# A gap of 64 bytes between the ring of the split weights and the activations

## The chip, the core and the metric

The kernel runs on one core of a Trainium2 chip. The metric is the device time of one execution in microseconds (us); lower is better. TensorE multiplies and writes to PSUM, VectorE, ScalarE and GpSimd work on vectors, and SyncE issues DMAs. A matmul has two operands in SBUF: the weights, 128 x 128 here, which an instruction of their own loads into the array, and the columns, 256 or 512 of them, which stream through it. Both lie at byte addresses within each of SBUF's 128 partitions, and those addresses are what this change is about.

## What is computed

```python
attn_out = _attn_ref(q, k, v, n_sink, window)          # 2 x 8 heads, 768 x 64, window 128, 4 sinks
x = attn_out.transpose(0, 2, 1, 3).reshape(1536, 512)
h = x @ w_in                                           # 512 -> 2048
y = (max(h, 0) + alpha * min(h, 0)) @ w_out            # 2048 -> 512
p = domain_probs / (domain_probs.sum(-1) + 1e-09)
out = sum(p[:, e] * (max(y @ w1[e], 0) @ w2[e]) for e in range(4))   # 512 -> 1024 -> 512
```

All arrays are float32. To keep that precision the kernel splits every operand of the feed-forward part into a high and a low half of a shorter float format (names ending in h and l) and makes three matmuls of one product: high by high, high by low, low by high.

## The kernel before

**Stages.** Attention runs over 32 pairs of a head with 256 queries, one per step p. From step 11 on, the first layer of the feed-forward part is interleaved with it by a hand-written list (`LEAD`): for units of 256 tokens and single blocks of 128 features, `s1` (x into the hidden block) and later `s2_transposed` (hidden block into the output). Each of the two is a burst of 12 matmuls of 256 columns. Then `rest` finishes the first layer: one more unit of 256 tokens, then the other blocks for chunks of 512 tokens, again 12 matmuls for `s1` and 12 for `s2_transposed`, now of 512 columns. Last come the experts. Their first pair of blocks goes through `s1` and `s2_natural`; the other 15 pairs go through `products`, which makes seven products of half size instead of eight: `four` for tokens 0 to 1023 (48 matmuls of 512 columns), `halves` for tokens 1024 to 1535 (42 matmuls of 256 columns), and then `out` (72 matmuls of 512 columns).

**Which operand is which.** In `s1` and `products` the weights of the matmul are slices of the split weights (`wh`, `wl`, and `th`, `tl` for sums of them), the columns are x (`xh`, `xl`, later called `yh`, `yl` in the same tiles) or sums of x (`s2h` and the like in pool `wide`; `s_wh`, `s_wl` in the trace are the sums for `halves`, which lie in the right-hand pools below). In `s2_transposed` the weights are again from `wh`, `wl`, the columns are the hidden block (`gha`, `gla`, `gh`, `gl`). In `s2_natural` and `out` it is the other way round: the weights of the matmul are slices of the hidden block (`hgh`, `hgl`), and the columns are the second half of `wh`, `wl`.

**Addresses.** They follow from the order and size of the tiles, and the compiled program has the same ones. Pools are stacked from the left. `base` ends at byte 33,792 of a partition, which is 264 x 128. Pool `accp` (called `work`) follows: three accumulators of 8,192 bytes, two tiles `cm` of 2,048, the ring of six `wh` and six `wl` of 4,096, then three `xh` and three `xl` of 8,192. On top of it lie `at` and `tmp` during attention (with `ptsb`, `p`, `v`, `gha`, `gla`), and later `wide` (sums of x, `gh`, `gl`, `hgh`, `hgl`). Every size and every slice used by a matmul of the feed-forward part is a multiple of 128, so all these operands begin at a multiple of 128 bytes. From the right end hang `top` with a pad of 32 bytes and, below it, the two pools `late`, which hold the weights of blocks 6, 7, 14 and 15 (line 119 decides: slot k % 8 of 6 or 7) and later `s_wh`, `s_wl`; and, during attention, `atk` with `qs`, `kh`, `kl`. All of these begin 64 bytes past a multiple of 128 (221,120, 225,216, 212,928 and 217,024 for the four weights' tiles). The small tiles `ident` and `warm` in `base` begin 32 bytes past one.

In this document the **distance** of a matmul is the start of its columns minus the start of its weights, modulo 128: 0 for two operands in the same half of 128 bytes, 64 for opposite halves.

Of the kernel before, what the change touches and what calls it, by code (L numbers as in the profile page):

```python
# [9 lines left out]
F32 = mybir.dt.float32  # L10
# [11 lines left out]
P = 128  # L22
# [32 lines left out]
class Body:  # L55
# [643 lines left out]
        nc.gpsimd.tensor_tensor(lo, x, hi.bitcast(F32), ALU.subtract)  # L699

    def new_x(self, c, name="x"):
        self.xh[c] = self.work.tile([P, DM // P, CH], F32R, tag="xh", name=f"{name}h{c}", bufs=NC)
        self.xl[c] = self.work.tile([P, DM // P, CH], F32R, tag="xl", name=f"{name}l{c}", bufs=NC)

# [349 lines left out]
```

## Time and profile before

| | us |
|---|---|
| median of 3 runs | 895.2 (894.92 to 896.19) |
| the profiled execution, whole | 895.68 |
| its span, first to last instruction | 893.9 |
| TensorE busy in it (4956 matmuls) | 881.4 |

The profile has one line per group of equal instructions, and a timeline with the start of each. TensorE's matmuls overlap: the duration of one (389 ns for 512 columns) counts from its first column to its last result, and the next one starts before that. What a matmul costs in a dense run is therefore not its duration but the **step**, the time from its start to the start of the next one, and steps are read from starts in the timeline. The granted clock of TensorE is 0.998 of full speed over the span.

### The profile page before, as it was taken

To read this page: it belongs to the slowest core of one execution; us is meant where nothing else is said; L and a number is where in the kernel's file an instruction comes from. 1 tells how busy PE (TensorE), PEld (TensorE's weight loads), DVE (VectorE), ACT (ScalarE), POOL (GpSimd) and SP (SyncE) were. 2 spreads that over 40 slices of the span, in tenths; PEclk is the share of its full clock that TensorE was granted. 3 is DMA by queue.
4 is the path that set the end of the run, shared out by engine and by line. 5 is a ranking of instruction groups with operands and counts; after the bars stand their busy time and mean duration, and the time that the engine had idled before them with its cause. 6 is when DMAs were issued, how large, how long until landed. Compare 5 with 4: busy or idle time off the path is not lost.

```text
span 893.9 us, 13192 instructions
## 1 busy us (share of the span) xinstructions
PE 881.4 (99%) x4956; PEld 747.4 (84%) x4956; DVE 560.0 (63%) x1104; ACT 330.8 (37%) x773; POOL 368.9 (41%) x349
## 2 busy tenths in 40 slices
PE   9999999999999999999999999999999999999997
PEld 6578899998888888888888888888888888888886
DVE  5778877657995553456655665665566556656654
ACT  4787766754431222233312321231233223212310
POOL 1366644535763454475224404421441344044210
PEclk9999999999999999999999999999999999999999
DMA  5754432302332020000011101101110111011003
GB/s 163 190 184 146 154 120 84 100 1 71 119 118 71 12 70 13 1 25 23 1 48 48 41 7 48 48 3 46 47 48 1 48 48 36 12 48 48 1 1 146
DMA packets 23722, 54.51 MB, mean 61 GB/s; under 512 B 3168, under 2 KB 3168, under 8 KB 23648
## 3 DMA queue, kind: packets, MB, share of 16 engines
q1 hardware_dynamic: 23504, 53.57, 19.0%
q8 instruction: 41, 0.67, 0.3%
q14 instruction: 33, 0.27, 0.1%
q10 hardware_dynamic: 144, 0.00, 0.0%
HBM read 50.42 MB, written 3.15 MB: 60 GB/s over the span
## 4 chain that ended last, share of the span: by engine, by line
PE 93%; DVE 4%; issue 1%; ACT 1%; POOL 0%; DVEq 0%; ACTq 0%; POOLq 0%
PE o L437 9%; PE o L436 9%; PE o L438 9%; PE h L374 5%; PE h L375 5%; PE h L376 5%; PE h L253 5%; PE h L254 5%; PE h L255 5%; PE o L262 5%; PE o L263 5%; PE o L264 5%; PE pv L676 3%; PE c L374 3%; PE c L376 3%; PE c L375 3%
## 5 line engine op out<-in xcount | busy, mean ns | idle before, releaser
L441 DVE SCALAR_TENSOR_TENSOR acc<-o,prob,acc 128x512 f32<-128x512 f32 x180 | 135.1, 751 | 100.3 <-PE o L438 100.3
L140 POOL TENSOR_TENSOR wl<-wraw,wh 128x512 fp32r<-128x512 f32 x60 | 76.6, 1297 | 280.8 <-ACT wh L139 280.8
L437 PE MATMUL o<-wl,hgh 128*128 128x512 f32 x240 | 93.5, 389 | 0.0
L438 PE MATMUL o<-wh,hgl 128*128 128x512 f32 x240 | 93.4, 389 | 0.0
L436 PE MATMUL o<-wh,hgh 128*128 128x512 f32 x240 | 93.4, 389 | 0.0
L253 PE MATMUL h<-xh,wh 128*128 128x256 f32 (+1 forms) x264 | 90.1, 341 | 0.0
L254 PE MATMUL h<-xl,wh 128*128 128x256 f32 (+1 forms) x264 | 87.6, 332 | 0.0
L255 PE MATMUL h<-xh,wl 128*128 128x256 f32 (+1 forms) x264 | 87.4, 331 | 0.0
L289 POOL TENSOR_TENSOR gl<-qk,gh 128x512 fp32r<-128x512 f32 (+1 forms) x36 | 49.5, 1375 | 70.9 <-ACT gh L288 68.7
L288 ACT ACTIVATE gh<-qk 128x512 fp32r<-128x512 f32 (+1 forms) x36 | 21.5, 598 | 122.5 <-DVE qk L287 119.8
L379 DVE TENSOR_TENSOR wraw<-h,wraw 128x512 f32<-128x512 f32 x45 | 31.1, 691 | 48.2 <-PE h L376 46.3
L382 ACT ACTIVATE wraw<-h 128x512 f32<-128x512 f32 x15 | 8.9, 596 | 140.7 <-PE h L376 140.7
L286 DVE TENSOR_SCALAR qk<-h,alpha 128x512 f32<-128x512 f32 (+1 forms) x36 | 25.3, 703 | 53.4 <-PE h L255 53.3
L263 PE MATMUL o<-gl,wh 128*128 128x512 f32 (+1 forms) x144 | 54.0, 375 | 2.5 <-POOL gl L289 2.5
L253 PEld LDWEIGHTS h<-xh,wh 128*128 128x128 f32 x264 | 49.9, 189 | 6.5 <-issue 1.7
L255 PEld LDWEIGHTS h<-xh,wl 128*128 128x128 f32 x264 | 49.9, 189 | 4.8
L254 PEld LDWEIGHTS h<-xl,wh 128*128 128x128 f32 x264 | 50.0, 189 | 4.5
L608 ACT ACTIVATE p<-p,nmax 128x288 f32<-128x288 f32 (+1 forms) x96 | 47.9, 501 | 15.8 <-DVE nmax L587 15.7
L262 PE MATMUL o<-gh,wh 128*128 128x512 f32 (+1 forms) x144 | 53.7, 373 | 0.0
L264 PE MATMUL o<-gh,wl 128*128 128x512 f32 (+1 forms) x144 | 53.4, 371 | 0.0
L438 PEld LDWEIGHTS o<-wh,hgl 128*128 128x128 f32 x240 | 45.0, 188 | 9.4
L436 PEld LDWEIGHTS o<-wh,hgh 128*128 128x128 f32 x240 | 45.0, 188 | 8.9
(209 smaller groups left out, 2440.7 us busy)
## 6 DMA issues: line engine op xcount, KB each, us to landing
wraw<-in_w SPq DMA_DIRECT2D x32, 512.0 KB, 3.6
wraw<-in_w SPq DMA_DIRECT2D x64, 256.0 KB, 2.9
qk<-in_qk SPq DMA_DIRECT2D x21, 352.0 KB, 3.0
v<-in_v SPq DMA_DIRECT2D x12, 256.0 KB, 3.4
out<-acc SPq DMA_DIRECT2D x12, 256.0 KB, 2.3
qk<-in_qk SPq DMA_DIRECT2D x8, 272.0 KB, 3.7
qk<-in_qk SPq DMA_DIRECT2D x11, 176.0 KB, 3.0
qk<-in_qk SPq DMA_DIRECT2D x8, 136.0 KB, 3.4
```

Source lines behind the costliest of these rows:

```text
L140: nc.gpsimd.tensor_tensor(lo, x, hi.bitcast(F32), ALU.subtract)
L253: mm(ps, wh[:, c], xh[:, dk, :], start=dk == 0, stop=False)
L254: mm(ps, wh[:, c], xl[:, dk, :], start=False, stop=False)
L255: mm(ps, wl[:, c], xh[:, dk, :], start=False, stop=dk == DM // P - 1)
L262: mm(outs[dt], wh[:, c], gh, start=first and begins[dt], stop=False, skip_group_check=True)
L263: mm(outs[dt], wh[:, c], gl, start=False, stop=False, skip_group_check=True)
L264: mm(outs[dt], wl[:, c], gh, start=False, stop=last, skip_group_check=True)
L374: mm(ps, bh[:, c], ah[:, d, :], start=first and d == 0, stop=False, skip_group_check=True)
L436: mm(ps, hh[:, n], wh, start=x == 0, stop=False)
L437: mm(ps, hh[:, n], wl, start=False, stop=False)
L438: mm(ps, hl[:, n], wh, start=False, stop=x == 1)
L441: nc.vector.scalar_tensor_tensor(acc, ps, self.prob[:, nt, e:e + 1], acc, ALU.mult, ALU.add)
```

## The change

A tile of 64 bytes is allocated right before the first tile of x, and never used. The branch runs once, for the first chunk of x. (`general` is the path for other masks, which isn't taken here.)

```diff
@@ -699,6 +699,9 @@
     def new_x(self, c, name="x"):
+        if name in "xg" and not self.xh:
+
+            self.work.tile([P, 16], F32, name="gap")
         self.xh[c] = self.work.tile([P, DM // P, CH], F32R, tag="xh", name=f"{name}h{c}", bufs=NC)
         self.xl[c] = self.work.tile([P, DM // P, CH], F32R, tag="xl", name=f"{name}l{c}", bufs=NC)
```

No instruction is added, removed or moved. Everything in `accp` from `xh` on, and all that is stacked on it (`at`, `tmp`, `wide`), moves up by 64 bytes. The accumulators, `cm`, the ring, `base` and everything on the right stay where they were.

## Rows read from the trace of the kernel before

**Rows 1.** The page: busy us (share) of engines; shares of the last chain by engine

```profile
PE 881.4 (99%) x4956; PEld 747.4 (84%) x4956; DVE 560.0 (63%) x1104; ACT 330.8 (37%) x773; POOL 368.9 (41%) x349
...
PE 93%; DVE 4%; issue 1%; ACT 1%; POOL 0%; DVEq 0%; ACTq 0%; POOLq 0%
```

**Rows 2.** TensorE by stage: stretch, busy us (instructions), granted clock, DMA share, GB/s

```profile
40.00:92.00 52.00, 49.89 (x400) 1.00 0.51 157
92.00:204.00 112.00, 112.00 (x988) 1.00 0.28 86
204.00:226.00 22.00, 19.55 (x163) 1.00 0.30 96
240.00:430.00 190.00, 190.00 (x838) 1.00 0.13 44
437.00:890.00 453.00, 451.48 (x2292) 1.00 0.11 37
```

**Rows 3.** Waits from 204 to 226 us: total us, times, longest

```profile
ACT gh L288 <- DVE qk L287: 6.7, 4, 2.1
...
PEld o L263 <- POOL gl L289: 3.1, 3, 1.1
```

**Rows 4.** Groups of matmuls by shape: busy us, mean ns of one, idle before

```profile
L437 PE MATMUL o<-wl,hgh 128*128 128x512 f32 x240 | 93.5, 389 | 0.0
...
L263 PE MATMUL o<-gl,wh 128*128 128x512 f32 x120 | 46.9, 391 | 0.0
...
L376 PE MATMUL c<-yh,wl 128*128 128x256 f32 x60 | 17.0, 283 | 0.0
...
L376 PE MATMUL c<-s_wh,tl 128*128 128x256 f32 x60 | 16.6, 277 | 0.0
```

**Rows 5.** Timeline of TensorE in the first layer: start us, duration us, matmul

```profile
251.47 0.39 PE L253 MATMUL h<-xh,wh 128*128 128x512 f32 x1
251.70 0.39 PE L254 MATMUL h<-xl,wh 128*128 128x512 f32 x1
...
254.22 0.39 PE L262 MATMUL o<-gh,wh 128*128 128x512 f32 x1
...
256.94 0.39 PE L253 MATMUL h<-xh,wh 128*128 128x512 f32 x1
...
259.69 0.39 PE L262 MATMUL o<-gh,wh 128*128 128x512 f32 x1
```

**Rows 6.** Timeline of one `halves`, 42 matmuls, and the start of `out`

```profile
466.82 0.28 PE L374 MATMUL c<-yh,wh 128*128 128x256 f32 x1
...
467.54 0.29 PE L374 MATMUL c<-s_wh,th 128*128 128x256 f32 x1
...
467.90 0.28 PE L374 MATMUL c<-s_wh,th 128*128 128x256 f32 x1
...
468.92 0.28 PE L374 MATMUL c<-yh,th 128*128 128x256 f32 x1
...
471.76 0.39 PE L436 MATMUL o<-wh,hgh 128*128 128x512 f32 x1
```

**Rows 7.** Timeline of one burst of 12 during attention, and two scores after it

```profile
153.52 0.36 PE L253 MATMUL h<-xh,wh 128*128 128x256 f32 x1
153.72 0.28 PE L254 MATMUL h<-xl,wh 128*128 128x256 f32 x1
...
154.91 0.28 PE L255 MATMUL h<-xh,wl 128*128 128x256 f32 x1
155.03 0.30 PE L573 MATMUL s<-kh,qs 128*128 128x288 f32 x1
155.17 0.30 PE L574 MATMUL s<-kl,qs 128*128 128x288 f32 x1
```

**Rows 8.** Groups of matmuls between 92 and 204 us, columns as in rows 4

```profile
L253 PE MATMUL h<-xh,wh 128*128 128x256 f32 x92 | 28.0, 304 | 0.0
L262 PE MATMUL o<-gha,wh 128*128 128x256 f32 x88 | 26.8, 304 | 0.0
...
L629 PE MATMUL pt<-ident,p 128*128 128x128 f32 x96 | 14.7, 272 | 0.0
```

## The prediction

> **What bounds the kernel now.** I read the page's engine shares and chain first [rows 1]: TensorE is busy for 881.4 of 893.9 us, and 93% of the chain of work that ended last lies on it. A busy TensorE doesn't say that it sets the pace in every stage, so the table by stage comes next [rows 2]. From 92 to 204 us, from 240 to 430 and from 437 to 890 it has no idle time worth naming (112.00 of 112.00, 190.00 of 190.00, 451.48 of 453.00): there a matmul that takes less time shortens the run. From 40 to 92 it idles 2.1 us, and from 204 to 226 it idles 2.5 us, where matmuls wait for GpSimd and ScalarE waits for VectorE [rows 3]; what TensorE gains in these two stretches I count as nothing, since those other engines are late next. The granted clock is 1.00 in every one of these stretches, the 2.4 GHz level.
>
> Then the step of a matmul, from the timelines. With both operands at distance 0, twelve matmuls of 512 columns start from 254.22 to 256.94 us [rows 5]: 2.72 / 12 = 226.7 ns. Matmuls of 256 columns in a settled run go from 153.72 to 154.91, ten in 1.19 us [rows 7]: 119 to 120 ns. The difference is 106.7 ns for 256 columns, 0.417 ns a column, so a step is 0.417 x columns + 13.3 ns. The columns themselves would need 213.3 and 106.7 ns. The 13.3 ns are paid by some 3,500 matmuls of the feed-forward part, about 47 us, and the change aims at them and nothing else.
>
> **What the distance does in the trace of before.** It already holds both kinds, since the right-hand pools lie 64 bytes off.
>
> 256 columns, distance 64: the matmuls on s_wh and s_wl in `halves`. After three steps of 120 ns (467.54 to 467.90), nine take 467.90 to 468.92 [rows 6]: 113.3 ns. That is 6.7 ns less than 120, half of the 13.3. The groups say the same: mean duration 277 ns against 283 for the same line on yh [rows 4].
>
> 512 columns, distance 64: blocks 6 and 7 (and 14 and 15) of the first layer, whose weights lie in the right-hand pools. Their `s1` bursts go from 251.47 to 254.22 and from 256.94 to 259.69 [rows 5], 2.75 us for twelve: 229.2 ns. That is 2.5 ns *more* than 226.7. The group that mixes 48 of these with 72 at distance 0 has 391 ns against 389 elsewhere [rows 4], the same sign.
>
> Both operands 64 bytes off, so distance 0 again: the scores with 288 columns step by 140 and about 135 ns [rows 7], 288 x 0.417 = 120 plus 13 to 20. So it is the distance that counts, not that one operand begins at 64.
>
> **The change part by part.** It adds no instruction. The unused tile costs no time. What moves is every operand from x upwards. The order of prices is by width.
>
> (a) 512 columns that go from distance 0 to 64. The counts follow from the loops (24 matmuls make a block for 512 tokens). `s1` and `s2_transposed`: 360 each, less 144 each for blocks 6, 7, 14, 15, leaves 432. First expert pair: 72 + 72. `four`: 15 x 48 = 720. `out`: 15 x 72 = 1080. Together 2,376, all in stretches where TensorE sets the pace. At 2.5 ns from the right-hand blocks: +5.9 us. For all but `out` and `s2_natural` the columns lie 64 bytes ahead of a multiple of 128 and the weights on it; in [rows 5] columns are on it and weights off; for `out` the weights move. I take the sign of the distance as of no weight, since 64 and -64 are the same modulo 128. That is the least certain step of the sum, and a rival takes the other side. The bounds of this price are +2.5 and, from the 256-column rows, -6.7 ns.
>
> (b) 512 columns that go from 64 back to 0: the 288 of blocks 6, 7, 14 and 15, whose x and hidden block now lie 64 off like their weights. 288 x -2.5 = -0.7 us.
>
> (c) `halves`, 15 times. Now 42 matmuls take 466.82 to 471.76 us, 4.94 us, and 18 of them are already at 64 [rows 6]. After, all 42 are: three entering steps of 120 and 39 of 113.3 give 4.78. 15 x -0.16 = -2.4 us.
>
> (d) Bursts of 12 during attention. Between 92 and 204 us there are 92 / 4 and 88 / 4, so 45 [rows 8]. One's ten inner steps take 1.19 us [rows 7]. At distance 64 they would take 1.13 if the lower step held at once, and 3 x 0.120 + 7 x 0.1133 = 1.15 if each burst entered as in [rows 6]. I take the middle, -0.047 us: 45 x -0.047 = -2.1 us. The bursts before 92 and after 204 count as nothing (above), but for two of the 256-token unit after 226, 24 x -6.7 ns = -0.2.
>
> (e) The rest of attention: probabilities, values and sinks also move, so that the transposes go from 32 to another odd 32, and the values keep their distance of 64. No row shows a transpose at another distance. It is bounded by the 6.7 ns either way that a step has moved anywhere above: 96 transposes of probabilities in the bound stretch [rows 8] would make +-0.6 us. I take 0, between the two.
>
> (f) VectorE, ScalarE and GpSimd read and write the moved tiles too. I cost this at nothing: TensorE hides these engines after 226 us, where VectorE is busy 560.0 us over the whole span [rows 1], and if that cover went in `out`, VectorE's additions would come next.
>
> Sum: +5.9 - 0.7 - 2.4 - 2.1 - 0.2 = +0.5 us. Against the profiled execution, 895.68 us, that is 896.2; it lies 0.5 above the median of 895.2, so the median should become 895.7. Gains of the narrow matmuls and losses of the wide ones nearly cancel.
>
> A page of the Trainium skill speaks against any effect. "TensorE: Matmul & The Clock Gate", section "Step-by-step: what each phase is for", says that TensorE reads SBUF through two independent ports, one for the streaming operand and one for the weights. By that rule neither the 113.3 nor the 229.2 ns could come from the distance, and the sum would be 0. The trace doesn't agree in so far as steps do differ with equal shapes; whether addresses cause it, only a run can tell.
>
> **The rivals.**
>
> 1. Wide matmuls lose and the narrow gain doesn't come: slower. The 113.3 ns are seen in runs of 9 steps on operands that lie in a right-hand pool far from the ring; the bursts of attention are short, start after transposes and may never leave the entering steps of 120, and yh lies elsewhere. Then (c), (d) fall away: +5.9 - 0.7 = +5.2, 900.4 us. It decides from where the narrow gain falls under about half its 6.7 ns. For it: the entering steps. Against: the gain is the same in all of the 15 `halves`.
>
> 2. The sign of the distance decides. The rows at -64 (columns off) are the narrow ones and gain, those at +64 (weights off by -64, columns on) are the wide ones and lose; width and sign can't be told apart in this trace. After the change `out` and `s2_natural`, 1,152 matmuls with weights at 64, are at -64: x -6.7 = -7.7 us. The other 1,224 wide ones are at +64: +3.1. Blocks 6, 7, 14, 15: -0.7. The narrow ones on x (360 + 540 + 24) are at +64 and lose 2.5 each: +2.3. Sum -3.0, 892.2 us.
>
> 3. All widths gain 6.7 ns and blocks 6, 7, 14, 15 are slow for another reason. 2,376 x -6.7 = -15.9, with (c), (d): -20.6, about 874.6 us. Rows 5 speak against it.
>
> 4. No effect: the differing steps belong to the right-hand pools, or to the phase in which they run, and not to the distance. 895.2 us. The scores [rows 7], all of it in a right-hand pool, with the usual 13 to 20 ns, speak against it. This is also what the rule of the independent ports gives.
>
> **How the numbers follow.** Forecast, the sum: 0.50. Its own range is 893.5 to 898, from a wide price of 2.0 to 2.5 ns (the reading of a start is good to 0.01 us in 2.75), (d) between -0.037 and -0.057, and (e). Rival 1: 0.20. Rival 2: 0.15. Rival 3: 0.05. Rival 4: 0.10. The least change that can be measured here is about 0.2%, 1.8 us. The forecast's own spread falls beyond that by about 0.06 below and 0.10 above. Faster: 0.06 + 0.15 + 0.05 = 0.26. Slower: 0.10 + 0.20 = 0.30. Same: 0.44. The range takes in rivals 1, 2 and 4 with a margin of the reading, 891 to 900.5, and leaves out rival 3 and the tails.
>
> **What would show each step.** In the changed kernel's timeline: `out` steps of 229 ns (a); of 220, rival 2 or 3; of 226.7, rival 4. `four` the same. Blocks 6 and 7 of the first layer at 226.7 (b). In `halves` 113.3 throughout after three steps, and a duration of 277 also on yh (c); 120, rival 1. The bursts of attention with ten inner steps of 1.13 to 1.15 us, and the stretch that ended at 204 us about 2 us earlier (d). The prediction fails if distance 64 means another thing when both operands come from the left-hand pools.

## The result, and the profile after

The changed kernel takes 907.4 us (907.0 to 908.4) against 895.7 beside it: a ratio of 1.0136, interval 1.0124 to 1.0149. The forecast was 895.7 with a range of 891 to 900.5; the time lies above the range, and the change costs about 12 us. The profiled execution took 906.98 us, 11.3 more than that of before.

The page of the changed kernel, engine shares and chain, as [rows 1]; then TensorE by stage, as [rows 2] (stretch, busy us and instructions of PE, its weight loads PEld, DVE, ACT and POOL, granted clock, DMA share, GB/s):

```profile
PE 892.3 (99%) x4956; PEld 745.1 (82%) x4956; DVE 560.8 (62%) x1104; ACT 330.9 (37%) x773; POOL 368.6 (41%) x349
...
PE 94%; DVE 3%; ACT 1%; issue 1%; POOL 0%; DVEq 0%; ACTq 0%; POOLq 0%
```

```profile
40.00:92.00 52.00, 49.75 (x402) 40.50 (x401) 42.01 (x120) 41.69 (x116) 33.05 (x33) 1.00 0.50 158
92.00:204.00 112.00, 112.00 (x1005) 103.65 (x1004) 76.70 (x235) 77.93 (x236) 54.65 (x62) 1.00 0.27 86
204.00:226.00 22.00, 19.24 (x150) 17.93 (x149) 19.16 (x30) 9.95 (x20) 12.88 (x14) 1.00 0.30 97
240.00:430.00 190.00, 190.00 (x826) 154.98 (x825) 108.56 (x156) 54.40 (x92) 101.67 (x76) 1.00 0.13 42
437.00:890.00 453.00, 453.00 (x2254) 379.01 (x2254) 264.82 (x434) 116.14 (x229) 145.12 (x140) 1.00 0.10 33
```

TensorE grew by 10.9 us (881.4 to 892.3) with the same 4956 matmuls, and the other engines by less than 1 us. The clock is at 1.00, the 2.4 GHz level, as before. In equal stretches fewer matmuls start: 2254 instead of 2292 from 437 to 890 us, 826 instead of 838 from 240 to 430; from 92 to 204 it is the other way, 1005 instead of 988. So attention gained a little, and both feed-forward parts lost.

Groups by shape in the changed kernel (busy us, mean ns of one, idle before), as [rows 4]:

```profile
L437 PE MATMUL o<-wl,hgh 128*128 128x512 f32 x240 | 94.6, 394 | 0.0
...
L263 PE MATMUL o<-gl,wh 128*128 128x512 f32 x120 | 47.0, 392 | 0.0
...
L376 PE MATMUL c<-s_wh,tl 128*128 128x256 f32 x60 | 16.8, 281 | 0.0
L376 PE MATMUL c<-yh,wl 128*128 128x256 f32 x60 | 16.7, 279 | 0.0
```

`out` has 394 ns instead of 389. The narrow matmuls on yh fell from 283 to 279, not to 277; those on s_wh, whose operands did not move, rose from 277 to 281.

The changed kernel's timeline (start us, duration us, matmul): the second and last of two bursts of 12 during attention as [rows 7], the borders of bursts in the first layer as [rows 5], and those of the stages after it as [rows 6]:

```profile
143.37 0.28 PE L263 MATMUL o<-gla,wh 128*128 128x256 f32 x1
...
144.50 0.28 PE L264 MATMUL o<-gha,wl 128*128 128x256 f32 x1
...
155.43 0.28 PE L263 MATMUL o<-gla,wh 128*128 128x256 f32 x1
...
156.61 0.28 PE L264 MATMUL o<-gha,wl 128*128 128x256 f32 x1
...
252.07 0.39 PE L262 MATMUL o<-gh,wh 128*128 128x512 f32 x1
...
254.83 0.39 PE L253 MATMUL h<-xh,wh 128*128 128x512 f32 x1
...
257.61 0.39 PE L262 MATMUL o<-gh,wh 128*128 128x512 f32 x1
...
458.19 0.40 PE L374 MATMUL h<-yh,wh 128*128 128x512 f32 x1
...
467.81 0.28 PE L374 MATMUL c<-yh,wh 128*128 128x256 f32 x1
...
472.76 0.39 PE L436 MATMUL o<-wh,hgh 128*128 128x512 f32 x1
...
489.56 0.40 PE L374 MATMUL h<-yh,wh 128*128 128x512 f32 x1
...
499.36 0.28 PE L374 MATMUL c<-yh,wh 128*128 128x256 f32 x1
```

The ten inner steps take 1.13 us in the first of these bursts and 1.18 in the second, at the same distance; 1.13 to 1.15 were forecast. Of the 44 whole bursts between 92 and 204 us, 10 are like the first and 34 like the second. Twelve wide matmuls on ring weights take 2.76 us (230.0 ns each), twelve on block 7, due back at 226.7, take 2.78 (231.7). After 458 us lie, from line to line, one `four` (42 wide matmuls, 9.62 us, 229.0 ns each), one `halves` (42 narrow ones, 4.95 us, 117.9), one `out` (72 wide ones, 16.80 us, 233.3) and the next `four` (9.80 us, 233.3). `out` is slower than any price the forecast had for it. And two `four`s at the same distances differ by 4.3 ns a step: the first two of the 15 are the cheaper ones, the other 13 take 233.3.

Means over all steps, start to start, put the 11.3 us in place. The distance is here, as from now on, the start of the columns minus the start of the weights, **modulo 256**, so that 192 is the prediction's -64; the experiments show why.

| matmuls | count | distance before, after | ns before, after | us |
|---|---|---|---|---|
| `out`, 512 columns | 1079 | 0, 192 | 226.9, 233.3 | +6.95 |
| `four`, 512 | 630 | 0, 64 | 226.7, 232.8 | +3.86 |
| first layer, ring blocks, 512 | 432 | 0, 64 | 226.7, 229.5 | +1.20 |
| first layer, blocks 6, 7, 14, 15, 512 | 288 | 64, 128 | 229.0, 231.8 | +0.82 |
| first expert pair, 512 | 144 | 0, 64 and 192 | 228.9, 234.2 | +0.76 |
| `halves` on yh, 256 | 360 | 0, 64 | 119.2, 118.2 | -0.36 |
| `halves` on s_wh, 256 | 270 | 192, 192 | 115.5, 117.5 | +0.55 |
| bursts beside attention, 256 | 864 | 0, 64 | 129.6, 128.0 | -1.34 |
| all other steps of TensorE | | | | -1.1 |

Both numbers of the first expert pair hold one wait of 0.3 us at its end; without it they are 226.6 and 232.1. The last row is not attention's. It lies in the first twelve matmuls of the program, which warm up on the tile `warm` in `base`; no gap here moves that tile. Before and after:

```profile
1.19 5.44 PE L236 MATMUL busy<-warm 128*128 128x256 f32 x12 [1.19 <-DVE warm L207]
...
1.18 4.31 PE L236 MATMUL busy<-warm 128*128 128x256 f32 x12 [1.18 <-DVE warm L207]
```

In the profiled executions of all the whole kernels here these twelve take 4.3 to 5.5 us, 4.3 with x alone moved by 64 bytes and 5.5 with 128 bytes, so this is a difference of executions and no part of the change's cost. The other steps, transposes, scores and values of attention, sum to the same within 0.02 us.

### The profile page after: what moved, and what is told of

It is laid out like the page before. It is cut to its first block, busy times and chain, and to the rows that moved or that the text cites. A ratio compares the mean times of both kernels' runs of the same rounds, so it can differ in the third digit from the quotient of the medians.

```text
span 905.2 us, 13192 instructions
## 1 busy us (share of the span) xinstructions
PE 892.3 (99%) x4956; PEld 745.1 (82%) x4956; DVE 560.8 (62%) x1104; ACT 330.9 (37%) x773; POOL 368.6 (41%) x349
## 4 chain that ended last, share of the span: by engine, by line
PE 94%; DVE 3%; ACT 1%; issue 1%; POOL 0%; DVEq 0%; ACTq 0%; POOLq 0%
PE o L438 9%; PE o L437 9%; PE o L436 9%; PE h L375 5%; PE h L374 5%; PE h L376 5%; PE h L253 5%; PE h L255 5%; PE h L254 5%; PE o L262 5%; PE o L263 5%; PE o L264 5%; PE pv L676 3%; PE c L374 3%; PE c L376 3%; PE c L375 3%
## 5 line engine op out<-in xcount | busy, mean ns | idle before, releaser
L437 PEld LDWEIGHTS o<-wl,hgh 128*128 128x128 f32 x240 | 44.9, 187 | 10.4
```

The lines of the kernel that those rows point to most:

```text
L437: mm(ps, hh[:, n], wl, start=False, stop=False)
```

## The experiments

The theory after the result: the step depends on the distance, but not modulo 128, and with its sign. The rivals: another moved operand pays (the columns x, the pools above), the period is 128 bytes and the price was only mis-sized, or the step belongs to the place in the program.

### Which of the moved parts pays

Three kernels with gaps at other places. In the first, 64 bytes lie before x and 64 more behind it:

```diff
     def new_x(self, c, name="x"):
+        if name in "xg" and len(self.xh) == 0 and not self.xl:
+            self.work.tile([P, 16], F32, name="gap")
         self.xh[c] = self.work.tile(...)
         self.xl[c] = self.work.tile(...)
+        if name in "xg" and len(self.xl) == 1 and not self.gapped:
+            self.gapped.append(self.work.tile([P, 16], F32, name="gap2"))
```

> A gap of 64 bytes before x and a second one behind it: x alone lies 64 bytes off, and all that is stacked above (pool wide, at, tmp) is back on multiples of 128. Theory A (each matmul pays by its own distance, -64 and 64 alike): the matmuls with x or y as columns step as in the changed kernel, about 233 ns in four (360 of 720), 229.5 in the first layer; out and the sums of x in wide are back at 226.7. Sum: 360 x 6.2 + 216 x 2.8 + 72 x 4.4 - 0.4 = +2.7 us, about 898.5. Theory B (only the sign matters: columns ahead of weights cost 2.5, behind cost 6.6): four on y at 229, sum about +1.3 us. Theory C (the step hangs on the run before, not on the matmul's own addresses): out, which starts after halves, steps above 226.7 too, and the total is above 900.

Measured: 906.4 us, 1.0127 (1.0110 to 1.0144). Theory A's 898.5 failed. By its addresses `out` stands at 128 here, and costs 232.4 ns a step. 128 is not 0.

In the second only the gap behind x is there:

> The gap lies behind x instead of before it: x keeps distance 0, the pools above it (wide, at, tmp) lie 64 bytes off. Theory A: out at 233.3 (+7.0 us for 1080), four on sums in wide 360 x 6.2 = +2.2, s2 of the first layer +0.6, first expert pair +0.4: about +10 us, 906, and the sum with the run that moves x alone gives the whole loss of 11.7. Theory B: out +7.0, four on sums +0.9: about 904. Theory C: the two partial moves don't add up to the whole.

Measured: 907.3 us, 1.0139 (1.0122 to 1.0156). `out` at 192 has 233.2 ns, as in the changed kernel. The losses of the two partial moves, 11.0 and 11.9 us, add up to twice the whole, as theory C had it; `out` pays in both, at 128 and at 192. And in `halves` no operand has moved here, yet the matmuls on s_wh rose from 115.5 to 117.7 ns: theory C is right in this too, a step depends on more than its own distance.

In the third the gap lies before the ring, so that the weights in it, x and everything above it move together:

```diff
+        accp.tile([P, 16], F32, name="gap")
```

> The gap lies before the ring: ring, x and all above move together by 64 bytes, so that every distance on the left is 0 again. Theory A: the ring's matmuls of 512 columns are back at 226.7 and the time at 895.7 or slightly less; blocks 6, 7, 14 and 15 (weights on the right, now the same half of 128 as x, though 128 apart in 256) are at 226.7 if the distance counts modulo 128, above 231 if modulo 256 (they were at 231.7 in the changed kernel). A theory that the absolute address of x counts, and not the distance, expects about 907.

Measured: 898.7 us, 1.0038 (1.0024 to 1.0052). `out` and `four` are back at 226.9 and 226.7 ns: one of its groups, and one of the first layer's,

```profile
L437 PE MATMUL o<-wl,hgh 128*128 128x512 f32 x240 | 93.5, 389 | 0.0
...
L262 PE MATMUL o<-gh,wh 128*128 128x512 f32 x120 | 47.2, 394 | 0.0
```

All of `out`'s operands lie 64 bytes off, and it costs nothing: it is the distance between the two. What is still lost (1.8 us in the profiled execution, which took 897.49) lies where a right-hand operand stayed: blocks 6, 7, 14 and 15 are now 128 apart and step by 232.8 ns (+1.1 us), and the ring blocks between them, which are at 0, went from 226.7 to 228.5 (+0.8); s_wh in `halves` is at 128 too, 118.9 ns (+0.9). The twelve matmuls at the start took 1.1 us less, as in the changed kernel.

### The period

The gap made 128 bytes, and 256 (one number of the diff: 32 and 64 instead of 16).

> The gap has 128 bytes instead of 64. If the distance counts modulo 128: no change, 895.7, steps of 226.7. If modulo 256, as the slow blocks 6, 7, 14 and 15 of the changed kernel suggest (231.7 ns with both operands 64 off, but 128 apart modulo 256): some 2,376 wide matmuls at about 231.7, +12 us, 907.

Measured: 909.7 us, 1.0159 (1.0142 to 1.0176). `out` 232.4, `four` 232.5, the first layer 232.5 ns. Modulo 128 nothing had changed, and it is the slowest of all.

> The gap has 256 bytes. Theory E (distance modulo 256): 895.4, steps of 226.7. Theory D (modulo 512): out and four at 230 to 234, 905 to 910.

Measured: 895.6 us, 0.9998 (0.9989 to 1.0008). Every class of the table has its step of before, to 0.1 ns but for the bursts beside attention. Groups of it:

```profile
L437 PE MATMUL o<-wl,hgh 128*128 128x512 f32 x240 | 93.5, 389 | 0.0
...
L263 PE MATMUL o<-gl,wh 128*128 128x512 f32 x120 | 46.9, 391 | 0.0
...
L376 PE MATMUL c<-yh,wl 128*128 128x256 f32 x60 | 17.0, 283 | 0.0
```

These are the numbers of [rows 4]. The period is 256 bytes.

### The price of each distance, by itself

Kernels that hold nothing but groups of matmuls, each group at one distance, with the weights' columns changing as in `s1` (two matmuls on one piece of weights, one on the next). Each of these kernels ran once; the granted clock is 1.00 from 20 us on, as in the whole kernels.

> A kernel of matmuls alone (it leaves out the whole computation): 60 matmuls in the split format with fixed weights (from 128 columns on, three slices in turn) for each distance from 0 to 512 bytes in steps of 16, first with 512 and then with 256 columns, TensorE drained between the groups, and four groups in which columns and weights are moved together by 16, 64, 128 and 256 bytes. The names of the tiles spell the distance. Theory D (only distance 0 modulo 512 is fast, as the run with 128 bytes suggests): 226.7 ns at 0 and 512 alone, 229 to 233.5 at all others; with 256 columns 120 at 0 and 113 to 119 elsewhere. Theory E (modulo 256): 226.7 at 256 too. Theory A (modulo 128): at 128, 256, 384 too. Groups moved together: 226.7 if the distance counts.

Timeline of it, matmuls 13 and 37 of four groups (the name of the group is the distance; 320 is 64 modulo 256):

```profile
19.66 0.39 PE L57 MATMUL w_zero<-xt,wt 128*128 128x512 f32 x1
...
25.10 0.39 PE L57 MATMUL w_zero<-xt,wt 128*128 128x512 f32 x1
...
77.30 0.39 PE L57 MATMUL w_sixtyfour<-xt,wt 128*128 128x512 f32 x1
...
82.79 0.39 PE L57 MATMUL w_sixtyfour<-xt,wt 128*128 128x512 f32 x1
...
192.95 0.39 PE L57 MATMUL w_onehundredninetytwo<-xt,wt 128*128 128x512 f32 x1
...
198.55 0.39 PE L57 MATMUL w_onehundredninetytwo<-xt,wt 128*128 128x512 f32 x1
...
308.67 0.40 PE L57 MATMUL w_threehundredtwenty<-xt,wt 128*128 128x512 f32 x1
...
314.27 0.40 PE L57 MATMUL w_threehundredtwenty<-xt,wt 128*128 128x512 f32 x1
```

24 steps take 5.44, 5.49, 5.60 and 5.60 us: 226.7, 228.8, 233.3 and 233.3 ns. The settled steps, in ns:

| distance | 512 columns | 256 columns |
|---|---|---|
| 0, 256, 512 | 226.7 | 120.0 |
| 64 | 228.9, and 233.3 at 320 | 117.8 |
| 128 | 232.8 | 118.7 |
| 192 | 233.3 | 113.3 |
| the other multiples of 16 | 231 to 235, once 226.7 (368) | 113.3 to 120 |

So the widths answer to 192 in opposite ways. The rows of before held wide matmuls only at 64 and narrow ones only at 192 [rows 5, 6]; a wide one at 192 wasn't in them. With both operands moved together by 64, 128 or 256 bytes the step is 226.7 ns, by 16 it is 231.1.

64 and 320, and 112 (231.1) and 368 (226.7), differ though they are the same modulo 256. So one distance can have more than one settled pattern. The same groups without draining TensorE between them:

> Matmuls alone again (the computation is left out), without draining: 48 each at distances 0, 256, 0, 128, 0, 64, 0, 448, 0, 32, 0, 480, 0, 16, 0, with 512 and then 256 columns. If a step hangs on the matmul's own distance, the groups at 0 are at 226.7 from the first on. If it hangs on the run before, the first few of each group, or the whole group, keep the step of the group before.

Distance 0 settled at 226.67 and 120.00 after every neighbour, but only after up to 12 entering steps. Two lines, matmul 1 and 13 of the group at 0 behind the one at 64:

```profile
82.52 0.40 PE L57 MATMUL w_zero<-xt,wt 128*128 128x512 f32 x1
...
85.29 0.39 PE L57 MATMUL w_zero<-xt,wt 128*128 128x512 f32 x1
```

These 12 took 2.77 us, 230.8 ns each. A burst of 12 at distance 0 that follows one at 64 has no settled part.

A finer map, the multiples of 4 that aren't multiples of 16, was to find a distance that is faster for both widths:

> Matmuls alone (the computation is left out), 45 at each distance from 4 to 252 bytes in steps of 4 that the coarse map left out, first with 512, then with 256 columns, drained between groups. If SBUF lines of 16 bytes or more decide, the steps follow the neighbours of the coarse map (229 to 235 for 512 columns; 113 near 112 and 192, 116 to 120 elsewhere for 256). If single elements matter, other fast distances show: a wide step below 226.7 anywhere would contradict the reading that 0 modulo 256 is the best for 512 columns.

Nothing is below 226.7 for 512 columns (226.7 also at 28, 60, 156, 188 and 252; 240 at 196), and nothing below 113.3 for 256 (115.6 at 28 and 236; 130 at 104).

### What ran before

> It leaves out the computation: only matmuls in groups of 48, one group straight after the other, each group at one distance (columns minus weights, in bytes, modulo 256 or shown beyond it). One settled step per distance: every group at 64 with 512 columns settles at 228.9 ns and every group at 192 with 256 columns at 113.3, whatever ran before. Several settled patterns: the groups at 64 (512 columns) split between about 229 and 233 by what ran before them, 320 and 368 repeat 64 and 112 where the group before is the same, and 256 columns at 192 reach 113.3 after a group at 0 but stay near 117.5 after a group at 64 or 192 with 512 columns.

All groups at 64 and 320 with 512 columns settled at 228.9 here: that part of the second theory's expectation failed. The rest held as far as it was run: 112 and 368 both settled at 231.1, and 256 columns at 192 took 113.3 or 117.8 by what ran before. A narrow group at 192 right behind a wide one at 192 was not among the groups; the kernel of the mirror image, below, has that order and speaks against the 117.5 expected for it. Timeline, matmuls 13 and 37 of two groups of 256 columns at 192, the first behind wide ones at 64, the second behind narrow ones at 0:

```profile
155.32 0.28 PE L57 MATMUL n_onehundredninetytwo<-xt,wt 128*128 128x256 f32 x1
...
158.15 0.28 PE L57 MATMUL n_onehundredninetytwo<-xt,wt 128*128 128x256 f32 x1
...
211.30 0.28 PE L57 MATMUL n_onehundredninetytwo<-xt,wt 128*128 128x256 f32 x1
...
214.02 0.28 PE L57 MATMUL n_onehundredninetytwo<-xt,wt 128*128 128x256 f32 x1
```

2.83 and 2.72 us for 24: 117.8 and 113.3 ns for the same addresses. The same two steps would explain s_wh in `halves` (115.5 to 117.5), whose operands didn't move: what ran before it did. The two `four`s above, of 229.0 and 233.3, have the two steps seen at 64 and 320; what picks one of them isn't shown.

### x alone moved

x and yh 64 bytes further, and 192 bytes behind them, so that all else keeps its distance:

```diff
+        if name in "xg" and not self.xh:
+            self.work.tile([P, 16], F32, name="gap")
         self.xh[c] = self.work.tile(...)
         self.xl[c] = self.work.tile(...)
+        if name in "xg" and not self.gapped:
+            self.gapped.append(self.work.tile([P, 48], F32, name="gap2"))
```

> Only x and yh lie 64 bytes further; everything above them is a multiple of 256 from where it was. Theory that columns minus weights modulo 256 counts: out keeps 226.7 ns, four on yh goes to 229 to 233, the first layer's bursts of 512 columns on x to 229 to 232, the blocks 6, 7, 14, 15 to 232, halves on yh to 117.8. With 720 x 0 to 6 ns on four that is +2 to +5 us, 898 to 900. Rival, that the steps belong to the pools or to the phases of the program: nothing moves with x, 895.5.

Measured: 898.4 us, 1.0040 (1.0024 to 1.0056), as the theory of the distance had it. `out` stays at 226.9 ns, `four` has 230.6. In `four`, yh is at 64 and the sums are at 0, in turns. The first twelve on sums:

```profile
459.59 0.40 PE L374 MATMUL h<-s2h,th 128*128 128x512 f32 x1
...
462.36 0.40 PE L374 MATMUL h<-yh,th 128*128 128x512 f32 x1
```

2.77 us, 230.8 ns each at distance 0: the same as the twelve entering steps above. Even matmuls that keep their distance pay when their neighbours lose it.

x and yh 28 bytes further, inside larger tiles, by the finer map free for wide matmuls and good for narrow ones:

```diff
+        o = 7
+        for x, t in ((self.xh, "h"), (self.xl, "l")):
+            x[c] = self.work.tile([P, DM // P * CH + 64], F32R, tag="x" + t, ...)
+            x[c] = x[c][:, o:o + DM // P * CH].rearrange("p (d n) -> p d n", d=DM // P)
```

> Only x and yh lie 28 bytes further. By the map of single distances: 512 columns at 28 keep 226.7 ns, 256 columns at 28 take 115.6 instead of 120, blocks 6, 7, 14, 15 (distance 92) about 232 instead of 229. So 540 narrow on yh x -3 = -1.6 us, 288 x +2.7 = +0.8, the bursts of attention up to -2: 893 to 895. Rival, that the map of groups does not carry over to bursts of 12 and 24 among other work: same or slower, 895.5 to 899, with four or out above 227.

Measured: 896.0 us, 1.0010 (1.0001 to 1.0020): the rival. The narrow gain came (`halves` on yh 116.2 instead of 119.2, -1.1 us; the expectation's 540 matmuls on yh are 360, as the table has them, so that -1.1 is all that was due), but the wide matmuls of `four` rose to 228.6 (+1.2 us) and those of the first layer's ring to 229.2 (+1.1). The map of long groups didn't hold for bursts that alternate.

### The mirror image: a gap of 192 bytes

Still open was whether the sign makes the price of `out`, or only the pattern that it entered. With 192 bytes (48 instead of 16 in the diff) `out` stands at 64, and `four` and the ring blocks at 192.

> The gap has 192 bytes, so everything from x upwards moves by 192: out has its columns 64 ahead of its weights (64 modulo 256, it had 192 with the gap of 64), four and the first layer's ring blocks have 192, and the blocks 6, 7, 14, 15 come to 0. Theory that the sign counts (the first step of the forecast failed because out stood at 192): out 228.9 ns, by the lower of the two settled patterns seen at 64, and then four 233.3, ring blocks 231 to 233, blocks 6, 7, 14, 15 at 227: out +2.4, four +4.8, ring +2.5, late -0.6, together about +9 us, 904 to 905. Rival, that the sign is of no weight and only the entry into one of two patterns counts: out 233.3 again and four 229 to 233, 907 to 909. Rival, that the price belongs to out's place and not to distances: out 233, four 232.8 as with 64, blocks 6, 7, 14, 15 at 232, 907.4.

Measured: 900.5 us, 1.0055 (1.0038 to 1.0072). Its timeline at the same borders as above:

```profile
459.51 0.39 PE L374 MATMUL h<-yh,wh 128*128 128x512 f32 x1
...
469.31 0.28 PE L374 MATMUL c<-yh,wh 128*128 128x256 f32 x1
...
474.07 0.39 PE L436 MATMUL o<-wh,hgh 128*128 128x512 f32 x1
...
490.55 0.39 PE L374 MATMUL h<-yh,wh 128*128 128x512 f32 x1
```

`four` 9.80 us, 233.3 ns; `halves` 4.76 us, 113.3; `out` 16.48 us, 228.9. Each of these stages took a step that the matmuls alone show for its new distance, and the two rivals fall by their own numbers: `out` is at 228.9 and not 233. For `out`, then, the sign decides. For `four` it made little difference: 233.3 here at 192, and 233.3 in 13 of 15 at 64 in the changed kernel. One part did not follow: blocks 6, 7, 14 and 15, now at 0, stayed at 229.0 instead of 227, in bursts of 12 between neighbours at 192. The time is 4 us better than the theory's 904 to 905. Its wide terms came as expected (`out` +2.2, `four` +4.2, ring blocks +2.8 us). What it had left out are the narrow ones: `halves` -2.5 us, the bursts beside attention -2.4. Here narrow matmuls at 192 follow wide ones at 192, and reach 113.3.

### A version meant to gain

Narrow columns at 192 where they meet few wide ones (the third chunk of x, and the hidden block of the bursts beside attention), the right-hand weights on a multiple of 256, the rest at 0:

```diff
-        self.pad = top.tile([P, 8], F32, name="pad")
+        self.pad = top.tile([P, 56], F32, name="pad")
...
-        late = [[pool.tile([P, 4, UN], F32R, tag=tag, ...)
+        late = [[pool.tile([P, 4 * UN + 64], F32R, tag=tag, ...)[:, 48:48 + 4 * UN]
...
+        o = 48 if c == 2 else 0
...
+            tmp.tile([P, 48], F32, name="gap")
```

> The third chunk of x (narrow columns) lies at -64, the late weights on a multiple of 256 while the sums of halves stay at -64, all other distances are 0 modulo 256. By the map: halves on yh 113.3 (-2.0), bursts of attention on the third chunk 113.3 to 115 (-1.2), late weights 229.0 to 226.7 (-0.7), the wide use of the third chunk +0.6: about -3.3 us, 892 us. Rival, that 113.3 depends on what ran before: halves stay at 117 to 120 and only the late weights gain, 894.8.

Measured: 894.9 us, 0.9993 (0.9984 to 1.0002): the rival's time, and no difference that can be told from none. The bursts beside attention gained 1.4 us, blocks 6, 7, 14 and 15 only 0.2, and the ring blocks lost 0.6. One `halves` of it:

```profile
465.48 0.28 PE L376 MATMUL c<-yh,wh 128*128 128x256 f32 x1
...
470.42 0.39 PE L438 MATMUL o<-wh,hgh 128*128 128x512 f32 x1
```

4.94 us for 42, 117.6 ns, with all 42 at 192, against 113.3 in the kernel of the mirror image. What ran just ahead of it was a `four` at 0, there one at 192. In no kernel here did `halves` reach 113.3 on yh while `four` kept 226.7.

## Why the prediction was wrong, point by point

**(a), 512 columns.** This is the step that failed, and it was called the least certain: "I take the sign of the distance as of no weight, since 64 and -64 are the same modulo 128". They aren't, the period is 256. `out` at 192 pays 6.4 ns and not 2.5, so +6.95 us where 2.7 were in the sum. That is shown by the mirror image, in which `out` at 64 pays 2.0 ns, near the 2.5 of the row that the forecast used. A second thing failed in the same step, which has nothing to do with the sign: one row was taken for the price of a distance that has two. `four` stands at 64 as the forecast thought, and pays 6.1 ns, 13 of its 15 executions in the dearer pattern of that distance: +3.86 us. It was counted with 15 x 48 matmuls; they are 15 x 42, as the groups show, so 720 x 2.5 = 1.8 us was in the sum. The first layer's ring blocks took 2.8 ns, 432 matmuls +1.2 us: this part was right. All of (a), the first expert pair with it, came to +12.8 us instead of +5.9.

The bounds were at fault too. The upper end for the wide price was the one row that existed, +2.5 ns; the narrow row, 6.7 ns, was taken as a bound for a gain only. Its size the other way would have put (a) at up to 2,376 x 6.7 = 15.9 us, and the range up to about 906. The upper end of the forecast's own range doesn't come out of its terms either: with the dearest of each they give about +1.5 us, 896.7 and not 898.

**(b), blocks 6, 7, 14, 15.** Forecast -0.7 us, measured +0.8. Their distance went from 64 to 128, which modulo 128 looked like 0. Wide matmuls at distance 128 take 231.7 to 233.0 ns in every kernel here that has them.

**(c), `halves`.** Forecast -2.4 us, measured +0.2. Its row, 113.3 ns, was read rightly, but it was a row of 192, and yh came to 64: 117.8 by itself, 118.2 in the kernel. On top of it s_wh rose from 115.5 to 117.5 without having moved, as it did where only the pools above x moved. In the mirror image the forecast of 4.78 us for one `halves` came true, with 4.76.

**(d), bursts of 12.** Forecast -2.1 us. The ten inner steps took 1.168 us in the mean of 44 bursts instead of 1.192: -0.024 and not -0.047 each, so -1.1. The sign was right. 34 of the bursts took about 117.8 ns a step, the step of 64 by itself; the other 10 took the forecast's 113.3, so that 256 columns at 64 have two patterns as well.

**(e) and (f).** The rest of attention's steps changed by less than 0.02 us, so the 0 of (e) was right; the -1.1 us of the table's last row are the twelve matmuls at the start, a difference of executions. The sign named under (d), a stretch that ends about 2 us earlier, would have been met by luck: the last matmul of attention outside the bursts starts at 203.28 instead of 205.79 us, but 1.1 of these 2.5 us are that start. VectorE, ScalarE and GpSimd changed their busy time by at most 0.8 us, as (f) had it.

**The sum.** Against the forecast's +0.5 us: (a) +6.9, (b) +1.5, (c) +2.6, (d) +1.0, the start -1.1, together 10.9 of the 10.8 us by which it missed; (d) here with the bursts outside the bound stretch.

**The rivals.** Rival 2 had the right doubt: width and sign couldn't be told apart in that trace. But it gave the wide matmuls at -64 the gain of the narrow ones, so it erred on the other side, 892.2. Rival 1 (900.4) had the narrow gain largely missing, which is so, for a reason that it didn't have. A wide loss of more than 2.5 ns at -64 was in no case. Rival 4 is excluded by the kernels with 64, 128 and 256 bytes, which differ in nothing but addresses. The rule of the Trainium skill that stood beside it ("TensorE: Matmul & The Clock Gate", "Step-by-step: what each phase is for": two independent ports for weights and columns) would have every distance alike; the runs here don't agree, 226.7 against 233.3 ns, and they decide.

**What stays open.** Why 256 bytes, and why 512 and 256 columns answer in opposite ways, no run shows. Nor what picks the pattern: two `four`s of the changed kernel step by 229, the others by 233.3, and of the matmuls alone one group took 233.3, at 320 and on an idle TensorE, while the group at 64 on an idle TensorE and all groups at 64 or 320 right behind other matmuls took 228.9.

## What to carry to other kernels

Where a trace shows two steps for equal shapes, find out from the addresses which property differs, and vary it alone, before its price is put on two thousand others: here width and sign were tied together, and the modulus was guessed. In this kernel columns and weights that start a multiple of 256 bytes apart gave the least step for 512 columns, and 64 bytes of padding between two groups of tiles cost 1.4%; whoever inserts a tile should look at what it does to all that is stacked on it. A step should be priced in runs as long as those of the kernel, since bursts of 12 hardly leave the entering steps.

## What the runs showed of the hardware

- The step of a matmul depends on the distance of its operands modulo 256 bytes: 226.7 to 240 ns for 512 columns, 113.3 to 130 for 256, at the 2.4 GHz level throughout.
- At 192 narrow matmuls reach their lowest step (113.3), and wide ones take 233.3.
- A run of matmuls alone settles into a repeating pattern after up to 12 steps. One distance can have two (228.9 and 233.3 for 512 columns at 64; 113.3 and 117.8 for 256 columns at 192). For 256 columns at 192 what ran before picks one; for 512 columns at 64 what picks isn't shown.
- Starts of both operands moved together by 64, 128 or 256 bytes cost nothing; by 16 they cost 4.4 ns a step (231.1). This is one group of matmuls each, at distance 0.
